# Hashing the first pair of heads with four 32x32 tiles on the array's diagonal

## The chip, the cores and the metric

The kernel runs on one core of one Trainium2 chip. The metric is the device time of one execution in microseconds; several executions of one kernel are summed up by their median.

## What is computed

The reference is hash-masked attention followed by a gated MLP. q, k and v have 4 batches, 8 heads, 768 positions and 64 columns, in fp32. A query and a key may meet only if their hashes agree: each is multiplied by a 64x6 projection, and the six signs are the bucket.

```python
q_bits = (np.einsum('bhsd,dk->bhsk', q, proj) > 0)
k_bits = (np.einsum('bhsd,dk->bhsk', k, proj) > 0)
mask = q_bucket[:, :, :, None] == k_bucket[:, :, None, :]
scores = np.where(mask, scale * np.matmul(q, k.transpose(0, 1, 3, 2)), -1e9)
x = softmax(scores) @ v           # then transposed to 3072 x 512
out = x + sigmoid(x @ w_res) * ((gelu(x @ w_gate) * (x @ w_val)) @ w_out)
```

## The kernel before

**Tiling.** Heads are taken two at a time as a *pair*: 16 pairs, four to a batch. One pair and side (0 for q, 1 for k) is a tile of 128 partitions by 12 chunks of 64 columns (`ld`); chunks 0 to 5 belong to the first head, 6 to 11 to the second. For the scores, each chunk is widened to 71 rows: 64 of data, six of the hash bits as plus or minus one half, and one constant, so that one matmul gives the score with the mask in it. These rows are built in `nat` (bf16, position on the partition) and turned to `aug` (column on the partition).

**Order.** All engines run in the order in which the program issues their instructions; nothing is rearranged by a scheduler. `PLAN` is that order for the first batch, written out by hand, one tuple a step. Its first steps, up to the slots `('S', 0)` and so on, are the start of the kernel. `S` issues one slot of scores: two PSUM banks filled by PE (L500) and one exponential on ACT (L511). There are nine slots a pair. Two PSUM buffers serve all slots in turn, so slot n waits for the exponential of slot n - 2. `V` issues the matmuls with v (L475). After the four pairs of a batch come the gate and value matmuls (L525) and the projections (L557, L571).

**The first pair's path.** Loads come by head on SP's queue (`load_head`, L179): q's first head, k's first, q's second, k's second. The other loads follow on the same queue (L161, L169).

- `cast` writes the 64 data columns of `nat` as bf16: on ACT at L261, on POOL at L263 (q) and L265 (k).
- `tr` (L273, DVE) transposes `ld` in blocks of 32x32 into `t32`: partition 32a + r then holds column r of half a head (32 columns) for the positions of partition group a.
- `hash_one` (L318, PE) multiplies `t32` in fp32 with `projs`. `projs` is block-diagonal, 128x128 for each of the two halves of the head: block a holds 32 rows of the projection in six columns, the rest is zero. Two matmuls, one for each half, sum up in PSUM; the profile shows two matmul instructions for each of them, since fp32 takes two passes.
- `bits_one` (DVE) transposes the sums back in blocks (L323) and writes the six bits into `nat` (L325).
- `turn` (L373, PE) transposes `nat`, chunk by chunk, into a PSUM tile (`pt`), and `copy` moves that to `aug`, on ACT (L379) or DVE (L381).

PLAN takes the first pair in pieces: hash calls for q's chunks 0:4, k's 0:2, k's 2:6, then, after the first `turn` steps, q's 4:6 and 6:12, and k's 6:12 after `('S', 1)`. The `copy` steps for k 0:2, q 0:4 and q 4:6 are on ACT, that for k 2:6 on DVE. The `turn` steps for q 0:4 and q 4:6 write one `pt` tile.

**Where the projection comes from.** It is loaded once, as 32 rows by two halves by six columns (`projn`, L184, on ACT's queue). `spread` (L219, L221) copies it four times into `projs` ('s', two copies on POOL and two on ACT) and four times into `projw` (on POOL). `projw` has the four blocks side by side in 24 of 32 columns. It serves the pairs from 1 on: `hash_mm` (L284) already puts several jobs into column tiles of the array, 128 rows by 32 columns each.

**Before all this** PE runs 52 short matmuls on constants (`fill`, L229), and ACT loads its table of the exponential (L194).

Of the kernel before, what the change touches and what calls it, by code (L numbers as in the profile page):

```python
# [9 lines left out]
FP32 = mybir.dt.float32  # L10
BF16 = mybir.dt.bfloat16
AF = mybir.ActivationFunctionType
# [3 lines left out]

PLAN = [
    ('load', 1, 0), ('load', 1, 1), ('load_v', 0), ('load', 2, 0), ('load_v', 1), ('load', 2, 1),
    ('load', 3, 0), ('proj', 's', 'pssp'), ('proj', 'w', 'pppp'), ('cast', 0, 1, 'p', 0, 6),
# [10 lines left out]
    ('vs', 0), ('load', 4, 0), ('load', 5, 1), ('load', 4, 1), ('load_v', 3),  # L30
    ('S', 0),
    ('S', 1), ('hash1', 0, 1, 6, 12, 'av'), ('bits1', 0, 1, 6, 12), ('turn', 0, 0, 6, 12, 'av'),
# [60 lines left out]
def kernel(  # L93
# [12 lines left out]
    nc = tc.nc  # L106
    B, H, S, D = q.shape
    NBITS = proj.shape[1]
    DMODEL = H * D
    DFF = moe_w_gate.shape[1]  # L110
    P = 128
# [24 lines left out]
    const = ctx.enter_context(tc.tile_pool(name="const", bufs=1))  # L136
# [38 lines left out]
    def load_head(p, side, hi, eng):  # L175
        b, hp = divmod(p, HP)
        if (p, side) not in raw:
            raw[p, side] = ld_pool.tile([P, HT, D], FP32, tag=f"ld{side}", name=f"ld{side}")
        eng.dma_start(raw[p, side][:, hi * T:(hi + 1) * T].rearrange("p t d -> p (t d)"),  # L179
                      (q, k)[side][b, 2 * hp + hi].rearrange("(p t) d -> p (t d)", t=T))  # L180

    load_head(0, 0, 0, nc.sync)
    projn = const.tile([32, 2, NBITS], FP32, name="projn")
    nc.scalar.dma_start(projn, proj.rearrange("(h r) n -> r h n", r=32))  # L184
    load_head(0, 1, 0, nc.sync)
    load_head(0, 0, 1, nc.sync)
    load_head(0, 1, 1, nc.sync)
# [4 lines left out]
    nc.vector.memset(eps_sb, EPS)  # L192
    table = const.tile([P, 1], BF16, name="table")
    nc.scalar.activation(table, warm[:, 0:1], AF.Exp)  # L194
    projs = const.tile([P, 2, P], FP32, name="projs")
    nc.gpsimd.memset(projs, 0.0)
    projr = const.tile([P, NBITS, D], FP32, name="projr")
    projw = const.tile([P, 2, 32], FP32, name="projw")
    nc.gpsimd.memset(projw, 0.0)
# [15 lines left out]

    def spread(dst, engs):
        for a, eng in enumerate(engs):
            if eng is nc.scalar:
                nc.scalar.activation(dst(a), projn, AF.Copy)  # L219
            else:  # L220
                eng.tensor_copy(dst(a), projn)  # L221

    wps, wpt = [sc_ps.tile([P, 1024], FP32, tag="sp", name=name) for name in ("wps", "wpt")]

# [17 lines left out]
    for s in range(3):  # L242
        n = KF // 3
# [11 lines left out]
    def cast(p, side, eng, c0=0, c1=HT):  # L255
        x = (p, side)
        scale = (1.0 / C) if side == 0 else 1.0
        sl = slice(c0, c1)
        dst = nat_of(x)[:, sl, 0:D]
        if eng is nc.scalar:  # L260
            nc.scalar.activation(dst, raw[x][:, sl], AF.Copy, scale=scale)  # L261
        elif side == 0:
            eng.tensor_scalar(dst, raw[x][:, sl], scale, 1.0, op0=ALU.mult, op1=ALU.mult)  # L263
        else:
            eng.tensor_copy(dst, raw[x][:, sl])  # L265

    t32, hsum, htok = {}, {}, {}
# [43 lines left out]
    def hash_one(p, side, c0, c1, tag):  # L311
        n, x = c1 - c0, (p, side, c0)
        if tag in ("w0", "w1"):
            hsum[x] = (wpt, wps)[int(tag[1])][:, 0:2 * n * 32].rearrange("p (i c n) -> p i c n", i=2, c=n)
        else:
            hsum[x] = (av_ps if tag == "av" else mm_ps).tile([P, 2, n, 32], FP32, tag=tag, name="hs1")
        for dh in range(2):
            nc.tensor.matmul(hsum[x][:, 0], projs[:, dh, :], t32[p, side][:, c0:c1, dh, :],  # L318
                             start=(dh == 0), stop=(dh == 1))

    def bits_one(p, side, c0, c1):
        hs = hsum[p, side, c0]
# [52 lines left out]
    def turned(p, side, c0, c1, eng):  # L375
        dst = aug[p, side][0:KA, c0:c1, :]
        pt = pts[p, side, c0 // T][0:KA, c0 % T:c0 % T + c1 - c0]
        if eng is nc.scalar:
            nc.scalar.activation(dst, pt, AF.Copy)  # L379
        else:  # L380
            eng.tensor_copy(dst, pt)  # L381
# [74 lines left out]
    def x_turn(b, hp):  # L456
        pt = mm_ps.tile([P, T, P], BF16, tag="f" if b == 0 else "r", name="pt")
        for t in range(T):
            nc.tensor.transpose(pt[:, t, :], x_tok[b][:, hp, t, :], ident)  # L459
        if hp == HP - 1:  # L460
            nc.scalar.activation(x_sb[b][:, hp, 0:2], pt[:, 0:2], AF.Copy)
            nc.vector.tensor_copy(x_sb[b][:, hp, 2:T], pt[:, 2:T])
        else:
            nc.vector.tensor_copy(x_sb[b][:, hp], pt)
# [124 lines left out]
    ENG = {"v": nc.vector, "s": nc.scalar, "p": nc.gpsimd}  # L589
# [113 lines left out]
    def first_gv(i):  # L703
        begun.append(gv_mm(0, 0, (wg, wv)[i], 0, KM - 1))

    STEP = dict(
        S=score, V=value, fill=fill, tr=tr,
        proj=lambda w, engs: spread(
            (lambda a: projs[32 * a:32 * a + 32, :, 32 * a:32 * a + NBITS]) if w == "s" else
            (lambda a: projw[32 * a:32 * a + 32, :, NBITS * a:NBITS * (a + 1)]),  # L710
            [ENG[e] for e in engs]),
        cast=lambda p, side, e, *c: cast(p, side, ENG[e], *c),
        hash1=hash_one,
        bits1=bits_one,
        turn=lambda p, side, c0, c1, tag: turn_pe(p, side, c0, c1, tag, POOLS[tag]),
        copy=lambda p, side, c0, c1, e: turned(p, side, c0, c1, ENG[e]),
# [4 lines left out]
        w=load_w, load=load, load_v=load_v, xturn=lambda hp: x_turn(0, hp),  # L721
# [10 lines left out]
    for s in range(NSLOT, LAST):  # L732
        p, c = divmod(s, NCH)
# [60 lines left out]
```

## Time and profile before

| | |
|---|---|
| time, median of 3 runs | 339.16 us (339.11 to 339.23) |
| span of the profiled execution | 337.24 us; some 1.9 us of a run lie around it |
| busy: PE, DVE, ACT, POOL | 332.7, 216.4, 213.8, 175.0 us |
| L318, hash of the first pair | 24 matmuls, 3.9 to 10.4 us |
| L284, hash of later pairs | 176 matmuls, from 11.7 us |
| fill, L229 | 52 matmuls, 0.84 to 4.03 us |

The profile is that of one execution; its own run time isn't listed beside the span. Times in it are us from the span's start. In a timeline, a row gives start, length, engine, line, operation, output and input with their shapes and a count; in square brackets stands how long the engine was idle before and what ended that. PE is the matmul, PEld the weight load that belongs to it. Ends of matmuls are modelled, so matmuls that follow one another overlap in the rows; the distance of two starts tells more than the length of one. The columns of the windows view are named where it is shown.

### The profile page before, as it was taken

What the parts mean: (1) busy time and instruction counts of PE and PEld (TensorE: products, weight loads), DVE (VectorE), ACT (ScalarE), POOL (GpSimd) and SP (SyncE); (2) the same over time, 40 slices, a digit from 0 to 9 for tenths busy, and PEclk for the clock granted to TensorE, in tenths of its full rate; (3) what the DMA queues carried; (4) which work ended last, traced back from release to release, by engine and by line L of the source; (5) the groups of instructions that cost most, each with busy time, mean ns of one, the idle gap of its engine ahead of it and who ended that gap; (6) DMA issues with size and microseconds to landing.
All of it is one profiled execution on the core that took longest, in us unless ns stands there. A gap on an engine that the chain in (4) does not pass through costs nothing.

```text
span 337.2 us, 7740 instructions
## 1 busy us (share of the span) xinstructions
PE 332.7 (99%) x3086; PEld 205.2 (61%) x3086; DVE 216.4 (64%) x458; ACT 213.8 (63%) x247; POOL 175.0 (52%) x260
## 2 busy tenths in 40 slices
PE   8999999999999999999999999999999999999996
PEld 8677666565666655665666665666566665666444
DVE  7977675664577958875687896876567444343243
ACT  4889962237999962437999982255999984322220
POOL 4779930234489942575999982567978100000000
PEclk9999999999999999999999999999999999999999
DMA  7998999999966233516149933923140340000012
GB/s 218 372 297 127 207 246 196 188 150 194 319 225 169 61 97 80 106 37 126 63 110 275 268 109 91 137 47 65 32 126 33 80 101 33 31 2 0 31 64 94
DMA packets 74387, 43.88 MB, mean 130 GB/s; under 512 B 52544, under 2 KB 71360, under 8 KB 74352
## 3 DMA queue, kind: packets, MB, share of 16 engines
q1 hardware_dynamic: 67872, 37.95, 45.6%
q0 software_dynamic: 6400, 5.44, 10.4%
q8 instruction: 24, 0.39, 0.5%
q14 instruction: 11, 0.09, 0.1%
q10 hardware_dynamic: 80, 0.00, 0.0%
HBM read 29.56 MB, written 6.29 MB: 106 GB/s over the span
## 4 chain that ended last, share of the span: by engine, by line
PE 93%; ACT 3%; DVE 1%; POOL 1%; issue 1%; DVEq 0%; ACTq 0%
PE sp L525 37%; PE fps L571 18%; PE sp L500 16%; PE av L475 9%; PE rps L557 6%; PE hs L284 3%; ACT ering L511 3%; PE wps L229 1%; PE hs L318 1%; POOL pr L335 1%; PE pt L373 1%; ACT e L511 1%; DVE sums L341 1%; PE pt L459 0%; DVE o L577 0%
## 5 line engine op out<-in xcount | busy, mean ns | idle before, releaser
L511 ACT ACTIVATE e<-sp 128x1024 bf16<-128x1024 f32 x117 | 117.7, 1028 | 8.5 <-PE sp L500 3.4
L335 POOL TENSOR_TENSOR pr<-ld,projr 128x384 f32<-128x384 f32 x96 | 93.9, 998 | 46.3 <-DVE sums L341 27.7
L542 ACT ACTIVATE gt<-sp 128x768 bf16<-128x768 f32 x48 | 38.9, 811 | 83.5 <-PE sp L525 77.9
L500 PE MATMUL sp<-aug,aug 71*128 71x256 bf16 (+1 forms) x384 | 86.0, 325 | 0.3
L571 PE MATMUL fps<-wo,hh 128*128 128x512 bf16 (+2 forms) x312 | 79.6, 362 | 0.0
L545 DVE TENSOR_TENSOR hh<-gt,sp 128x768 bf16<-128x768 bf16 x48 | 45.8, 954 | 44.1 <-PE sp L525 40.8
L525 PE MATMUL sp<-x_sb,wg 128*128 128x512 bf16 (+1 forms) x384 | 70.9, 326 | 0.0
L525 PE MATMUL sp<-x_sb,wv 128*128 128x512 bf16 (+1 forms) x384 | 70.9, 326 | 0.0
L475 PEld LDWEIGHTS <-e 128*128 128x128 bf16 x936 | 43.5, 97 | 25.9
L341 DVE TENSOR_REDUCE sums<-pr 128x6 f32<-128x384 f32 x96 | 50.0, 541 | 11.5 <-POOL pr L335 11.0
L525 PEld LDWEIGHTS <-wg 128*128 128x128 bf16 x384 | 37.1, 98 | 25.6 <-issue 1.2
L525 PEld LDWEIGHTS <-wv 128*128 128x128 bf16 x384 | 37.5, 98 | 24.9 <-issue 0.2
L475 PE MATMUL av<-va,e 128*128 128x65 bf16 x936 | 47.0, 193 | 0.0
L571 PEld LDWEIGHTS <-hh 128*128 128x128 bf16 x312 | 28.1, 97 | 22.0 <-issue 0.2
L500 PEld LDWEIGHTS <-aug 71*128 71x128 bf16 x384 | 29.2, 97 | 11.1 <-issue 2.0
L574 DVE SCALAR_TENSOR_TENSOR fps<-th,fps 128x512 f32<-128x512 f32 (+2 forms) x26 | 17.0, 653 | 26.2 <-PE fps L571 26.0
L557 PE MATMUL rps<-wr,x_sb 128*128 128x512 bf16 x96 | 27.1, 379 | 0.0
L511 ACT ACTIVATE ering<-sp 128x1024 bf16<-128x1024 f32 x27 | 25.8, 1031 | 1.7 <-PE sp L500 1.4
L561 ACT ACTIVATE th<-rps 128x512 f32<-128x512 f32 x24 | 14.2, 594 | 18.5 <-PE rps L557 18.5
L273 DVE STREAM_TRANSPOSE t<-ld 128x768 f32<-128x768 f32 (+3 forms) x28 | 23.1, 844 | 0.7 <-PE hs L284 0.6
L454 DVE COPY av<-av 128x390 f32<-128x390 f32 x24 | 13.5, 563 | 11.9 <-PE av L450 11.7
L263 POOL TENSOR_SCALAR nat<-ld 128x768 bf16<-128x768 f32 (+1 forms) x12 | 9.6, 805 | 20.0 <-DMA aug<-nat 17.4
(76 smaller groups left out, 259.7 us busy)
## 6 DMA issues: line engine op xcount, KB each, us to landing
ldv<-in_v_dram SPq DMA_DIRECT2D x16, 384.0 KB, 5.6
out_dram<-o SPq DMA_DIRECT2D x23, 256.0 KB, 2.4
ld<-in_q_dram SPq DMA_DIRECT2D x15, 384.0 KB, 5.7
ld<-in_k_dram SPq DMA_DIRECT2D x15, 384.0 KB, 6.0
wg<-in_moe_w_gate_dram POOLq DMA_DIRECT2D x4, 384.0 KB, 9.1
wv<-in_moe_w_val_dram POOLq DMA_DIRECT2D x4, 384.0 KB, 10.2
wo<-in_moe_w_out_dram POOLq DMA_DIRECT2D x3, 512.0 KB, 7.5
wr<-in_moe_w_res_dram POOLq DMA_DIRECT2D x1, 512.0 KB, 15.7
```

The source lines that it names most:

```text
L273: nc.vector.transpose(t32[p, side][:, sl].rearrange("p c h n -> p (c h n)"), raw[p, side][:, sl].rearrange("p c d -> p (c d)"))
L335: nc.gpsimd.tensor_mul(pr, raw[x][:, hi * T:(hi + 1) * T], projr[:, bit].unsqueeze(1).to_broadcast([P, T, D]))
L341: nc.vector.reduce_sum(sums[x][:, hi * T:(hi + 1) * T, bit], pr, axis=mybir.AxisListType.X)
L475: nc.tensor.matmul(av[p, hi][:, qt, :], e[:, off:off + P], va[:, hi, jt, 0:D + 1], start=first, stop=(repeats(p, hi) and jt == T - 1), ski ...
L500: nc.tensor.matmul(sp[:, off:off + nq * P], ks[0:KA, hi * T + jt, :], qs[0:KA, hi * T + qt0:hi * T + qt0 + nq, :], start=True, stop=True)
L511: nc.scalar.activation(e, sp, AF.Exp, scale=float(ALPHA))
L525: nc.tensor.matmul(sp[:, c0:c1], w[:, kk, bass.ts(m, P)], xs[:, kk, c0:c1], start=(kk == 0), stop=(kk == KM - 1))
L542: nc.scalar.activation(gt, sp[:, 0:S], AF.Gelu)
L545: nc.vector.tensor_mul(hidden[b][:, m, :], gt, ps[1][:, 0:S])
L557: nc.tensor.matmul(rps, x_sb[b][:, kk, t, :], wr[:, kk, :], start=(kk == 0), stop=(kk == KM - 1))
L571: nc.tensor.matmul(fps[:, cs], hh[:, m, bass.ts(t, P)], wo[:, m, cs], start=(m == 0), stop=(m == KF - 1))
L574: nc.vector.scalar_tensor_tensor(fps[:, cs], th[:, cs], 1.0, fps[:, cs], op0=ALU.add, op1=ALU.mult)
```

## The change

`hash_one` no longer multiplies with a block-diagonal 128x128 matrix. For each half of the head it issues four matmuls of 32x32 weights, tile a at rows 32a and columns 32a of the array, each reading its own 32 partitions of `t32` and writing its own 32 partitions of the sums. The projection is loaded in four copies, one to each group of 32 partitions (`projc`), by two loads on ACT's queue, one for each half; their source repeats the same rows four times. `projs`, its memset and its four spread copies are gone. POOL's copies into `projw` now read `projc`, and come behind the cast of k's chunks 0:6 on POOL. The ACT cast of k's chunks 6:12 moves from its place ahead of the first copies to behind the copy of q's chunks 4:6, just ahead of slot 0.

```diff
-    ('load', 3, 0), ('proj', 's', 'pssp'), ('proj', 'w', 'pppp'), ('cast', 0, 1, 'p', 0, 6),
+    ('load', 3, 0), ('cast', 0, 1, 'p', 0, 6), ('proj', 'pppp'),
     ('cast', 0, 0, 'p', 6, 12), ('tr', 0, 0, 0, 4), ('cast', 0, 0, 's', 0, 6), ('fill', 4, 70),
-    ('cast', 0, 1, 's', 6, 12), ('tr', 0, 1, 0, 2), ('cast', 1, 0, 'p'), ('tr', 0, 0, 4, 6), ('fill', 44, 70),
+    ('tr', 0, 1, 0, 2), ('cast', 1, 0, 'p'), ('tr', 0, 0, 4, 6), ('fill', 44, 70),
...
-    ('bits1', 0, 0, 6, 12), ('tr', 1, 0), ('copy', 0, 0, 4, 6, 's'), ('tr', 1, 1), ('load', 5, 0),
+    ('bits1', 0, 0, 6, 12), ('tr', 1, 0), ('copy', 0, 0, 4, 6, 's'), ('cast', 0, 1, 's', 6, 12), ('tr', 1, 1), ('load', 5, 0),
...
-    projn = const.tile([32, 2, NBITS], FP32, name="projn")
-    nc.scalar.dma_start(projn, proj.rearrange("(h r) n -> r h n", r=32))
+    projc = const.tile([P, 2, 32], FP32, name="projc")
+    for h in range(2):
+        nc.scalar.dma_start(projc[:, h, 0:NBITS], bass.AP(tensor=proj.tensor, offset=proj.offset + 32 * NBITS * h,
+                                                          ap=[[0, 4], [NBITS, 32], [1, NBITS]]))
...
-    projs = const.tile([P, 2, P], FP32, name="projs")
-    nc.gpsimd.memset(projs, 0.0)
+    nc.gpsimd.memset(projc[:, :, NBITS:32], 0.0)
...
-            if eng is nc.scalar:
-                nc.scalar.activation(dst(a), projn, AF.Copy)
-            else:
-                eng.tensor_copy(dst(a), projn)
+            eng.tensor_copy(dst(a), projc[32 * a:32 * a + 32, :, 0:NBITS])
...
         for dh in range(2):
-            nc.tensor.matmul(hsum[x][:, 0], projs[:, dh, :], t32[p, side][:, c0:c1, dh, :],
-                             start=(dh == 0), stop=(dh == 1))
+            for a in range(0, P, 32):
+                nc.tensor.matmul(hsum[x][a:a + 32, 0], projc[a:a + 32, dh, :], t32[p, side][a:a + 32, c0:c1, dh, :],
+                                 start=(dh == 0), stop=(dh == 1), tile_position=(a, a))
```

More of the change, by code (lines that the diff above doesn't have):

```diff
@@ L707 @@
         S=score, V=value, fill=fill, tr=tr,
[L708 to L711, printed above, removed]
+        proj=lambda engs: spread(lambda a: projw[32 * a:32 * a + 32, :, NBITS * a:NBITS * (a + 1)],
+                                 [ENG[e] for e in engs]),
         cast=lambda p, side, e, *c: cast(p, side, ENG[e], *c),
```

## The prediction

> **What bounds the kernel now.** I read the page first, then the busy time by stage.
>
> ```profile
> span 337.2 us, 7740 instructions
> PE 93%; ACT 3%; DVE 1%; POOL 1%; issue 1%; DVEq 0%; ACTq 0%
> ```
> ```profile
> 0.00:8.53 8.53, 7.68 (x85) 7.63 (x85) 6.03 (x23) 3.71 (x8) 3.65 (x18) 1.00 0.76 219
> 8.53:23.70 15.17, 15.13 (x208) 10.54 (x208) 12.68 (x29) 13.10 (x15) 11.44 (x21) 1.00 1.08 348
> 23.70:45.00 21.30, 20.93 (x319) 14.40 (x316) 14.24 (x35) 21.21 (x23) 20.01 (x35) 1.00 0.96 191
> 45.00:337.20 292.20, 288.97 (x2489) 172.64 (x2485) 183.49 (x373) 175.76 (x202) 139.93 (x188) 1.00 0.50 112
> ```
>
> The columns are stretch, length, busy PE, PEld, DVE, ACT, POOL, then clock, DMA share, GB/s. PE looks full everywhere, so the sum says little. The change touches only the first hash, before about 10 us. Behind it ACT is full until 45 us (21.21 of 21.30), and PE after that. Nothing after the start has slack to take up a shift, so the end moves by what the first exponentials move. I therefore look for what sets them, on ACT's timeline:
>
> ```profile
> 7.09 0.52 ACT L261 ACTIVATE nat<-ld 128x384 bf16<-128x384 f32 x1 [2.91 <-DMA ld<-in_k_dram]
> 7.52 0.85 ACT L379 ACTIVATE aug<-pt 71x256 bf16<-71x256 bf16 x2
> L379 ACT ACTIVATE aug<-pt 71x512 bf16<-71x512 bf16 x1 | 0.6, 582 | 0.0
> 8.73 0.38 ACT L379 ACTIVATE aug<-pt 71x256 bf16<-71x256 bf16 x1 [0.36 <-PE pt L373]
> 9.16 3.99 ACT L511 ACTIVATE ering<-sp 128x1024 bf16<-128x1024 f32 x4
> 14.33 1.02 ACT L511 ACTIVATE ering<-sp 128x1024 bf16<-128x1024 f32 x1 [0.91 <-PE sp L500]
> ```
>
> This is the real chain before the first exponential (S0, 9.16). The cast of k's second head waits 2.91 us for a load, two copies (7.52 to 8.37) stand behind it, the transposes of q's chunks 4 and 5 reuse the bank those copies read, and the third copy (8.73) follows them. At the same time PE is nearly as late: I call the six hash calls A (q 0:4), B (k 0:2), C (k 2:6), D (q 4:6), E (q 6:12), F (k 6:12).
>
> ```profile
> L318 PEld LDWEIGHTS wps<-t,projs x4: 333/333/333, 5.5 to 6.2; 128*128 128x128 f32 x4
> L318 PE MATMUL wps<-t,projs x4: 397/421/527, 5.6 to 6.4; 128*128 128x128 f32 x4
> L318 PEld LDWEIGHTS wpt<-t,projs x4: 190/192/192, 6.9 to 7.2; 128*128 128x128 f32 x4
> L318 PE MATMUL hs<-t,projs x16: 314/354/550, 3.9 to 10.1; 128*128 128x192 f32 x8, 128*128 128x128 f32 x4, 128*128 128x64 f32 x4
> ```
> ```profile
> 3.91 1.94 PE L318 MATMUL hs<-t,projs 128*128 128x128 f32 x8
> 5.54 0.97 PEld L318 LDWEIGHTS wps<-t,projs 128*128 128x128 f32 x4
> 6.60 0.52 PE L373 MATMUL pt<-ident,nat 128*71 128x128 bf16 x6
> L373 PE MATMUL pt<-ident,nat 128*71 128x128 bf16 x54 | 4.6, 220 | 0.1
> 6.91 0.53 PEld L318 LDWEIGHTS wpt<-t,projs 128*128 128x128 f32 x4
> 7.41 0.87 PE L318 MATMUL hs<-t,projs 128*128 128x192 f32 x4
> 8.11 0.58 PE L373 MATMUL pt<-ident,nat 128*71 128x128 bf16 x6
> ```
>
> Each call is four passes (two halves of the head by two passes of fp32). C's weight loads (333 ns each, 0.97 for four) are (0.97 - 0.33)/3 = 0.213 us apart; D's (191 ns, 0.53) only (0.53 - 0.19)/3 = 0.113. The same load takes half the time after about 6.6 us, although the granted clock reads 1.00 throughout: PE is slow until then, and A, B and C lie in the slow part. A 64-column pass lasts 314 ns and a 128-column one 421, so 64 columns stream in 0.107 us and 128 columns in 0.213 there. A 128-column pass is thus bound by its data as much as by its weights; only B and D, 64 columns wide, are bound by weights.
>
> **The change part by part.** First, do four diagonal tiles run together? No such matmul is in the trace. The nearest are the column tiles of the later hash:
>
> ```profile
> 21.61 0.37 PE L284 MATMUL hs<-t,projw 128*32 128x192 f32 x4
> 21.61 0.53 PE L284 MATMUL hs<-t,projw 128*32 128x192 f32 x8
> L284 PE MATMUL hs<-t,projw x176: 326/326/350, 11.7 to 207.1; 128*32 128x192 f32 x176
> ```
>
> Four matmuls of 350 ns each fit into 0.37 us, so they run side by side, and the next four end 0.16 us later: a pass of 192 columns costs 0.162 us however many tiles share it. I take the same for diagonal tiles, with a pass bound by its data alone: 0.213 (128 columns, slow), 0.107 (64, slow), about 0.056 (64, fast), 0.162 (192, fast). Bounds: no gain for B and D if 32-column weights come no faster than 128-column ones; four times each pass if the tiles run one after another.
>
> Second, PE changes its tiling. Here the rows show the price:
>
> ```profile
> 21.30 0.38 PE L500 MATMUL sp<-aug,aug 71*128 71x512 bf16 x1
> 13.25 0.49 PE L284 MATMUL hs<-t,projw 128*32 128x192 f32 x4
> 13.68 0.61 PE L500 MATMUL sp<-aug,aug 71*128 71x256 bf16 x3
> ```
>
> Six transposes of 128 bf16 columns, 220 ns each, lie (0.52 - 0.22)/5 = 0.06 apart, the later ones 0.056; 512 columns stream in 0.22. What follows the matmul at 21.30 could start at 21.52; the tiled hash starts at 21.61: 0.09 on the way in. Of the four at 13.25 the last two start at 13.25 + 0.16 and end streaming at about 13.58; S4 starts at 13.68: 0.10 on the way out. The first weights after a switch also lie bare (350 against 326 ns), so I charge 0.12 a switch, up to 0.2 in the slow part. Blocks ABC, DE and F make six switches; four lie ahead of S0, but the first replaces A's own bare weight load (550 against 421 ns, 0.13) and counts nothing.
>
> The sum on PE up to S0: B saves 4 x 0.107 = 0.43. C then ends streaming at 6.17 instead of 6.60. The bits that the first transposes need are no later:
>
> ```profile
> 5.51 0.18 DVE L325 TENSOR_SCALAR nat<-hs 128x24 bf16<-128x24 f32 x1
> 5.89 0.27 DVE L323 STREAM_TRANSPOSE hs<-hs 128x64 f32<-128x64 f32 x1 [0.20 <-PE hs L318]
> 6.19 0.17 DVE L325 TENSOR_SCALAR nat<-hs 128x12 bf16<-128x12 f32 x1
> 6.28 0.57 DVE L273 STREAM_TRANSPOSE t<-ld 128x384 f32<-128x384 f32 x1
> 7.91 0.17 DVE L325 TENSOR_SCALAR nat<-wpt 128x12 bf16<-128x12 f32 x1
> ```
>
> A's bits end at 5.51 + 0.18 = 5.69, and B's transpose waits 0.20 for PE. That wait goes; DVE starts an instruction some 0.08 before the last one's end (its next one after 6.19 + 0.17 begins at 6.28), so B's steps move from 5.89 to 5.61 and its bits are ready at 6.08. Transposes start at 6.17 + 0.15 to 0.2 = 6.36, still slow up to 6.6, and end streaming at 6.81 (before, 6.60 + 6 x 0.056 + 0.02 = 6.96). D starts at 6.93, four passes of 0.056 end at 7.15. E, 192 columns, gains nothing: 4 x 0.162 to 7.80. With the switch the next six transposes run from 7.93 to 8.26, S0 behind them: 8.26 instead of 8.53 (8.11 + 0.58 - 0.22 + 0.06), **0.27 us earlier on PE**. D's bits come at 7.83 (7.91 + 0.17 less 0.25), just in time.
>
> Now ACT. The cast at 7.09 leaves its place, so the first two copies no longer wait for the load (from about 6.7 to 7.6, not 7.52 to 8.37), and the reuse of their bank holds nothing up. The third copy hangs on PE and comes 0.27 earlier, at 8.46. But the cast now stands between that copy and the exponential. One copy of this size holds the next off by 0.27 (the second of the two at 7.52 ends at 8.37 and lasts 0.58, so it starts at 7.79), the cast by 0.43 (7.09 to 7.52). Exponential S0 starts at 8.46 + 0.27 + 0.43 = 9.16; its scores are ready at 8.26 + 0.22 + 0.38 = 8.86. **It starts when it starts now.** The stall on the load is gone, and the work that stood in it is late next. S1 starts 0.27 earlier on PE, F's two switches eat 0.24 of it, S2 is 0.03 earlier. S4 at 14.33 waits for PE's later hash, which follows S3, which waits for exponential S1's buffer: again set by S0. Sum: 0.0, with 0.1 either way for the slow switches.
>
> What costs nothing, and its cover:
>
> ```profile
> 0.80 0.41 ACTq L184 DMA_DIRECT2D projn<-in_proj_dram  x1
> 1.25 1.28 ACT L194 ACT_TABLE_LOAD   x1 [1.25 <-PEq L778]
> 3.65 0.87 POOL L221 COPY projw<-projn 32x12 f32<-32x12 f32 x4
> 5.39 0.51 POOL L263 TENSOR_SCALAR nat<-ld 128x384 bf16<-128x384 f32 x1 [0.30 <-DMA ld<-in_q_dram]
> projn<-in_proj_dram ACTq DMA_DIRECT2D x1, 1.5 KB, 2.3
> ld<-in_k_dram SPq DMA_DIRECT2D x2, 192.0 KB, 3.7
> ```
>
> The second projection load adds 0.41 on ACT's queue, so the table load ends at 2.95, before A at 3.91; the two ACT spread copies that follow go, and the cast of q's first half behind them is wanted only at 6.36. On POOL the cast of k's first half steps ahead of the four projw copies (0.87): even if that half lands as late as the slower row says, at 5.0, its 0.5 is done before 6.36, and projw is first read at 11.7. POOL's two projs copies and the larger memset go. SP's order stays. The projection landed 2.3 us after issue; the second load, issued at 1.21, would land at 3.5 by that, at 4.9 by the slower row. The first load is wanted at 3.9, the second at A's third pass, 4.47. I take the nearest row, 2.3: no wait; by the other end A is 0.4 to 0.6 late. The moved cast's output is read by the transposes of k 6:12, which stand behind the hash at 11.7, 2.5 us after it.
>
> **The rivals.** *Tiles one after another (slower).* The change would then not do what it says. Passes cost four times: A lasts to 7.0 (twelve slow, four fast), B 0.89, C 1.71, D 0.89, E 2.59, with the transposes and switches S0 comes near 14.1 and its exponential at 15.0; F adds 1.9 between S1 and S2. In all 7.8: 347.0 us. Against it speak the column tiles above; for it, that no row has tiles on different rows of the array. The Trainium skill, "TensorEngine Tiling (Array Packing)", Restrictions and Gotchas, says that different row tiles can't use one PSUM bank at the same time, and the diagonal tiles all write one bank; by that rule this is the case, and no row here shows it.
>
> *PE stays slow longer (slower).* PE left the slow rate at 6.6 after running full. With a quarter of the array at work and switches between, it might leave it later. If the slow rate lasted through S0: six transposes 0.64, D 0.43, E 1.28, six more 0.64 and three switches put the last one's end at 9.8 and the exponential at 10.5: +1.4, 340.6 us; a part of it if the delay is shorter. The Trainium skill, "TensorE: Matmul & The Clock Gate", Part 1, ties full clock to a busy window of about 3.4 us that starts anywhere; the trace's 6.6 agrees with such a rule, though the clock row doesn't show it.
>
> *PE turns fast sooner (faster).* Today the load at 7.09 holds the start whatever PE does; afterwards nothing but PE and DVE does. If PE is fast from 4.3, q's second head (landed by 5.39) is transposed by 6.1, the bits of C and D follow by 7.0, the last transposes by 7.6, exponential at 8.3: -0.85, 338.3 us.
>
> *Weights or the load bind.* 32-column weights no faster (B +0.43, D +0.22) or a late projection: +0.6, 339.8 us.
>
> **How the numbers follow.** The span is 337.24 and the median 339.16; the 1.9 us around the span stay. Forecast: 339.1 us, chance 0.57, its own range 338.9 to 339.4. Fast sooner 0.15, weights or load 0.09, slow longer 0.10, one after another 0.09. The range takes in the forecast, fast sooner, the 0.6 and the lesser half of slow longer: 338.2 to 340.3. About 0.2% (0.7 us) is what a measurement of this kernel can tell from no change. Over that on the fast side is half of fast sooner and a little: 0.09; on the slow side one after another, slow longer and a share of the 0.6: 0.22; within: 0.69.
>
> **What would show it.** Right: diagonal matmuls in groups of four that start together; B's passes near 0.11; S0's first matmul near 8.3; the cast between the third copy and the exponential, which starts at 9.1 to 9.2; no ACT wait on a load near 7. Wrong: passes four times as long, an fp32 pass that doesn't halve near 6.6, or an exponential S0 off by more than 0.3. If S0 moves and the end doesn't follow, the chain behind it is misread.

## The result, and the profile after

The changed kernel takes **345.09 us** (median of four runs, 342.42 to 349.10) where the kernel before takes 339.13 on the same chip: ratio 1.0148, 95% interval 1.0112 to 1.0184. One run, 349.10, had PE's clock granted at 0.979 and is left out of the ratio. The forecast was 339.1, the range 338.2 to 340.3: the result lies outside it, on the slow side. The profiled execution took 344.37 us, with a span of 342.3 instead of 337.2.

First the page of the changed kernel: the span, the packets of two queues, and the chain by engine.

```profile
span 342.3 us, 7880 instructions
q8 instruction: 25, 0.41, 0.5%
q10 hardware_dynamic: 264, 0.01, 0.0%
PE 78%; POOL 11%; ACT 3%; DMA 2%; DVE 2%; issue 1%; ACTq 0%; POOLq 0%; DVEq 0%
```

The page of the kernel before has for the same two queues:

```profile
q8 instruction: 24, 0.39, 0.5%
q10 hardware_dynamic: 80, 0.00, 0.0%
```

DMA is now in the chain, q10 (ACT's loads of the projection) carries 264 packets instead of 80, and the engines' own loads of instructions, q8, are one more. All three will matter. Next the chain of waits up to the first exponential (start, length, what):

```profile
0.81 1.18 ACTq L185
1.99 0.03 issue
2.02 5.34 DMA projc<-in_proj_dram
7.36 0.02 issue
```

The projection's second load is issued at 2.0 and lands at 7.36. PE shows what it does meanwhile (start, length, what, and in brackets the idle time before and what ended it):

```profile
3.99 0.65 PE L317 MATMUL hs<-t,projc 32*32 32x128 f32 x8
7.40 0.64 PE L317 MATMUL hs<-t,projc 32*32 32x128 f32 x24 [2.76 <-DMA projc<-in_proj_dram]
8.96 0.83 PE L372 MATMUL pt<-ident,nat 128*71 128x128 bf16 x6 [0.32 <-POOL nat L261]
10.14 1.50 PE L317 MATMUL hs<-t,projc 32*32 32x192 f32 x16
```

A's two passes on the first half run at 3.99, the third waits until 7.40. The second loss stands in the last two rows: six transposes take 0.83 us where they took 0.52, and the sixteen tiles of E 1.50. PE is at half speed again. The windows view (stretch, length, busy PE, PEld, DVE, ACT, POOL, granted clock, DMA share, GB/s) shows it in the clock:

```profile
4.30:7.40 3.10, 0.34 (x9) 0.00 (x1) 0.59 (x3) 0.20 (x1) 0.29 (x1) 1.00 0.95 289
8.10:11.40 3.30, 2.98 (x54) 1.74 (x42) 2.44 (x10) 0.97 (x2) 3.08 (x7) 0.51 1.06 371
```

PE idles for most of 3.1 us, then the granted clock is 0.51 for 3.3. The same view with finer bounds:

```profile
4.78:8.19 3.41, 0.79 (x36) 0.79 (x40) 0.41 (x2) 0.00 (x0) 0.57 (x4) 1.00 0.96 305
8.19:11.60 3.41, 3.09 (x51) 1.68 (x43) 2.35 (x10) 0.97 (x2) 3.23 (x7) 0.50 1.06 366
```

The clock falls at 8.19, not when PE goes idle (2.76 us, up to 7.40) and not when it starts again, and it is back at 11.60. From 7.40 to 8.19 PE ran at the fast spacing, 0.11 us for a pass of 128 columns. On ACT, the rows up to the first exponential:

```profile
12.14 0.38 ACT L378 ACTIVATE aug<-pt 71x256 bf16<-71x256 bf16 x1 [1.73 <-PE pt L372]
12.42 0.51 ACT L259 ACTIVATE nat<-ld 128x384 bf16<-128x384 f32 x1
12.83 1.01 ACT L510 ACTIVATE ering<-sp 128x1024 bf16<-128x1024 f32 x1
```

It starts at 12.83 instead of 9.16: **+3.67**. Of these, 2.93 are A's third pass (7.40 instead of 4.47). The rest of the path, 0.74 longer, has the slow spell in it. Up to the end of the third batch the shift stays at 3.65; between batches three and four 0.25 comes on top (which I didn't follow), and DVE's last result is 3.89 later. But the span is 5.08 longer, so **the tail behind DVE's last result grew by 1.19**, from 2.50 to 3.69 us. The waits of SP's queue in the changed kernel name a part of it:

```profile
SPq L786 <- DMA out_dram<-o: 1.2, 1, 1.2
```

In the kernel before the same row reads 0.3.

### The profile page after: what moved, and what is told of

Read it like the earlier page. It is cut to its first block, busy times and chain, and to the rows that moved or that the text cites. A ratio compares the mean times of both kernels' runs of the same rounds, so it can differ in the third digit from the quotient of the medians.

```text
span 342.3 us, 7880 instructions
## 1 busy us (share of the span) xinstructions
PE 333.4 (97%) x3158; PEld 203.3 (59%) x3158; DVE 216.3 (63%) x458; ACT 213.1 (62%) x245; POOL 174.4 (51%) x258
## 4 chain that ended last, share of the span: by engine, by line
PE 78%; POOL 11%; ACT 3%; DMA 2%; DVE 2%; issue 1%; ACTq 0%; POOLq 0%; DVEq 0%
PE sp L524 36%; PE fps L570 13%; PE sp L499 12%; POOL pr L334 7%; PE av L474 7%; PE rps L556 5%; PE hs L282 3%; ACT ering L510 3%; DMA projc<-in_proj_dram 2%; POOL v L393 1%; PE pt L372 1%; POOL va L385 1%; DMA x_sb<-x_tok 1%; ACT e L510 1%; PE hs L317 1%
## 5 line engine op out<-in xcount | busy, mean ns | idle before, releaser
L541 ACT ACTIVATE gt<-sp 128x768 bf16<-128x768 f32 x48 | 38.9, 810 | 83.8 <-PE sp L524 78.2
L453 DVE COPY av<-av 128x390 f32<-128x390 f32 x24 | 13.5, 564 | 11.9 <-PE av L449 11.7
L419 DVE TENSOR_TENSOR x_tok<-av,rec 128x384 bf16<-128x384 f32 x32 | 17.8, 558 | 1.1
```

The lines of the kernel that those rows point to most:

```text
L419: nc.vector.tensor_mul(x_tok[b][:, hp, :, hi * D:(hi + 1) * D], o[:, 0:T, 0:D], rec.unsqueeze(2).to_broadcast([P, T, D]))
L541: nc.scalar.activation(gt, sp[:, 0:S], AF.Gelu)
```

## The experiments

**Theory:** the four-copy loads land late, since a load whose slowest dimension is 4 goes to four DMA engines. PE then idles and falls to half speed, and the end of the program costs another 1.2 us. **Rivals:** the tiles themselves are slow; many small pieces land late however they are dealt; POOL's new order holds PE.

All versions:

| kernel | first exponential | tail | median | ratio to before, 95% |
|---|---|---|---|---|
| before | 9.16 | 2.50 | 339.13 | |
| the change | 12.83 | 3.69 | 345.09 | 1.0148 (1.0112 to 1.0184) |
| e1 tiles, old load | 8.61 | 3.53 | 340.07 | 1.0029 (1.0019 to 1.0039) |
| e1p the same, cast on POOL | 8.27 | 2.84 | 339.52 | 1.0011 (1.0002 to 1.0020) |
| e2 new load alone | 14.87 | 3.41 | 345.62 | 1.0193 (1.0180 to 1.0207) |
| e3 change, four loads | 11.21 | 3.92 | 343.07 | 1.0098 (1.0063 to 1.0134) |
| e4 change, PE kept busy | 13.07 | 3.30 | 343.94 | 1.0162 (1.0125 to 1.0198) |
| e5 e1p with long fillers | 8.22 | 2.49 | 338.78 | 0.9992 (0.9983 to 1.0001) |
| e6 before, one more load | 9.00 | 3.29 | 339.87 | 1.0030 (1.0017 to 1.0043) |
| e7 before, cast moved | 9.43 | 2.47 | 339.13 | 1.0006 (0.9997 to 1.0014) |
| e9 change, POOL's order | 12.71 | 4.01 | 344.97 | 1.0205 (1.0155 to 1.0254) |
| e11 before, more fillers | 9.49 | 2.47 | 340.36 | 1.0038 (1.0024 to 1.0051) |
| e12 change, other rows | 8.88 | 3.94 | 340.41 | 1.0040 (1.0027 to 1.0053) |

The tail is the time from the end of DVE's last result to the end of the span. First exponential and tail are us of the one profiled execution, the median is that of all runs. The ratio is to the kernel before on the same chip (338.88 to 339.16).

### e2: the new load without the tiles

```diff
-    projn = const.tile([32, 2, NBITS], FP32, name="projn")
-    nc.scalar.dma_start(projn, proj.rearrange("(h r) n -> r h n", r=32))
+    projc = ...          # the change's two loads; projs is filled from it
```

> The kernel before with its 128x128 block-diagonal hash and its cast in place, with one thing of the change: the projection comes in four copies by the two loads, and the block-diagonal weights are copied from those. Theory 'landing': the hash can't start before some 7.4 us, all six calls late, first exponential 12 to 14 us, time 342 to 346, and the executions spread by several us. Theory 'tiles': 339 to 339.5 us.

345.62 us. With the old 128x128 weights the loss is all there, so the tiles don't cause it. Its page has the same packets. In its timeline PE waits for POOL's copy of the projection, which itself waited for the load until 7.32, and its windows show the same clock:

```profile
q10 hardware_dynamic: 264, 0.01, 0.0%
```
```profile
7.82 1.95 PE L320 MATMUL hs<-t,projs 128*128 128x128 f32 x8 [3.79 <-POOL projs L223]
```
```profile
7.40:14.40 7.00, 6.58 (x33) 6.26 (x34) 3.12 (x11) 2.33 (x7) 5.92 (x15) 0.51 1.03 365
```

Here the half clock lasted for 6.8 us, from 7.6 to 14.4.

### e1 and e1p: the tiles on the old load

```diff
-    ('load', 3, 0), ('cast', 0, 1, 'p', 0, 6), ('proj', 'pppp'),
+    ('load', 3, 0), ('proj', 's', 'pssp'), ('cast', 0, 1, 'p', 0, 6), ('proj', 'w', 'pppp'),
...
-    for h in range(2):
-        nc.scalar.dma_start(projc[:, h, 0:NBITS], ...)
+    nc.scalar.dma_start(projn, proj.rearrange("(h r) n -> r h n", r=32))
```

e1p also takes the moved cast off ACT: `('cast', 0, 1, 'p', 6, 12)` behind POOL's cast of the next pair.

> Keeps the 32x32 tiles and the moved cast, but loads the projection once as before (64 pieces of 24 B) and copies it on POOL and ACT into the four groups of partitions. Theory 'landing' (the time is lost because the two four-copy loads land at 7.4 us instead of 3.1): hash starts at 3.9 to 4.0, first exponential at 9.1 to 9.3, time 338.9 to 339.5, and the executions agree to 0.3 us again. Theory 'tiles' (diagonal tiles and switches cost the time themselves): first exponential past 11, time 342 or more.

> As the one before, and the moved cast (k's chunks 6:12) goes to POOL, behind the cast of the second pair's q, so ACT has nothing between the third copy and the first exponential. If the prediction's sum was right (0.27 us gained on PE, eaten by this cast): first exponential near 8.9 instead of 9.16, time 338.7 to 339.0, 0.2 to 0.3 less than the run with the cast on ACT. If the cast is not what holds the exponential: no difference between the two.

The first exponential is 0.55 and 0.89 earlier than before, and yet the times are 340.07 and 339.52. The tails are 1.03 and 0.34 us longer, which gives back all that e1 gained. For e1p it is not the whole account: its profiled run took 338.84, 0.7 less than its median, and what the others spent isn't shown. The difference between the two is 0.55 us, more than expected; of the 1.29 us by which their profiles differ 0.69 lie in the tail. Of the tiles, e1's timeline shows:

```profile
6.60 0.83 PE L319 MATMUL hs<-t,projc 32*32 32x192 f32 x16
```

Sixteen tiles of 192 columns in 0.83 us: (0.83 - 0.32) / 3 = 0.17 us for each group of four, one tile's length 0.32. They run four together: in a group the starts lie 0.007 us apart.

### e12: the same pieces, dealt otherwise

```diff
-        nc.scalar.dma_start(projc[:, h, 0:NBITS], bass.AP(tensor=proj.tensor, offset=proj.offset + 32 * NBITS * h,
-                                                          ap=[[0, 4], [NBITS, 32], [1, NBITS]]))
+        nc.scalar.dma_start(projc[:, h, 0:NBITS], bass.AP(tensor=q.tensor, offset=q.offset + 32 * h,
+                                                          ap=[[D, P], [1, NBITS]]))
```

> The changed kernel with its two loads of 128 pieces of 24 bytes taken from 128 rows of q instead of four copies of the projection, so that the hash is of other numbers (its bits aren't the reference's, and what follows from them); pieces, bytes, queue and place stay. Theory (the copies' outer dimension of 4 deals each load to four engines, and its issue takes 1.18 us): dealt over 16 engines, 8 pieces each, with 256 pieces and 32 writes of semaphores on q10; second load landed at 4.0 to 5.0 instead of 7.36, first exponential 9 to 11, 339.5 to 342 us. Rival (any load of 128 small pieces lands that late, whatever its engines): landed 6.5 to 7.5, first exponential 12 to 13, 344 to 345.5 us.

The view of the DMA issues (packets of the queue; then bytes and time from issue to landing), and ACT's timeline:

```profile
q10 hardware_dynamic: 288, 0.01, 0.0%
projc<-in_q_dram ACTq DMA_DIRECT2D x2, 3.0 KB, 2.3
```
```profile
0.81 0.88 ACTq L185 DMA_DIRECT2D projc<-in_q_dram  x2
8.46 0.51 ACT L259 ACTIVATE nat<-ld 128x384 bf16<-128x384 f32 x1
8.88 1.01 ACT L510 ACTIVATE ering<-sp 128x1024 bf16<-128x1024 f32 x1
```

Landed 2.3 us after issue, 0.88 us for both issues instead of 1.75, first exponential at 8.88, better than expected. The theory stands, against the rival of the small pieces. How the dealing is read: of the 264 packets 256 are pieces of 24 bytes and 8 are semaphore writes of 4 bytes, four for each of the two loads; here there are 32, sixteen for each. In the changed kernel the second load's four writes come at 4.34, 4.78, 4.92 and 7.03 us: three were done before 5, and one was late. In e2, e4 and e9 two of the four come after 5.9. Here all 32 lie between 2.21 and 3.14. The Trainium skill, "DMA: Bandwidth & Descriptors", "Why a DMA increments its semaphore by 16 and not by 1", says that each engine that takes part in such a DMA writes to its semaphore once, and that the DMA goes to the largest number of engines, up to 16, that divides the slowest dimension of both sides; by that, a leading dimension of four copies allows four. The 8 and 32 writes agree.

So the landing, with the shorter issue, is worth some 4 us: 3.7 by the two ratios to the kernel before (1.0148 and 1.0040), 4.2 at DVE's last result in the two profiles (338.63 and 334.42). What is left over the kernel before, 1.25 us by the medians, comes with a first exponential that is 0.28 *earlier*: it is all tail (3.94 against 2.50).

### e3: four loads of 32 partitions

```diff
-    for h in range(2):
-        nc.scalar.dma_start(projc[:, h, 0:NBITS], ...)
+    for a in range(0, P, 32):
+        nc.scalar.dma_start(projc[a:a + 32, :, 0:NBITS], proj.rearrange("(h r) n -> r h n", r=32))
```

> The changed kernel, with the four copies brought by four loads of 32 partitions each (source and destination both 32 rows, 64 pieces of 24 B each, 256 in all as in the change) on ACT's queue. Theory 'four engines' (a load whose source begins with a repeat of four is dealt out to 4 of the 16 DMA engines, 32 pieces in a row on each, between the big loads' pieces): each of the four runs on 16 engines, the last lands near 4.5 us, first exponential 9.2 to 9.8, time 339.2 to 340. Theory 'pieces' (256 small pieces land late whoever carries them): the last lands past 6.5, time 342 or more.

```profile
q10 hardware_dynamic: 320, 0.01, 0.1%
projc<-in_proj_dram ACTq DMA_DIRECT2D x4, 1.5 KB, 3.1
```

256 pieces and 64 writes: sixteen engines a load. The loads landed a median of 3.1 us after issue, but they are issued one after another (0.45 each), so the last tile gets its weights at 5.66. PE runs A in fits and stays slow to 9.3; first exponential 11.21. The landing lies between the two expectations, and the time, 343.07 us, is the rival's: the dealing is right, but the landing is still too late for A. These loads read the same 32 rows four times, as the change does, so reading the same rows again is not what lengthens 3.1 us to the change's 5.3.

### e4: PE kept busy until the load lands

```diff
-    ('tr', 0, 1, 2, 6), ('hash1', 0, 0, 0, 4, 'av'),
+    ('tr', 0, 1, 2, 6), ('fill', 85, 70), ('hash1', 0, 0, 0, 4, 'av'),
```

> The changed kernel with 85 more filler matmuls of 70 columns ahead of hash A, so that PE doesn't idle from 4.3 to 7.4 us while it waits for the projection. Theory (PE falls back to half speed after an idle stretch): PE is fast from about 7 us on and stays so, C's and D's passes and the transposes behind 8.1 us come at the fast spacing (0.056 us for 128 columns of bf16), and the first exponential starts at about 11.7 instead of 12.83. The 170 added instructions also move PE's instruction loads (queue q8, 256 instructions each): the load that fell at 337.5, among the last output transfers, would come some 15 us earlier, and the issue of the second-to-last output DMA take 0.33 us instead of 0.66. Together 1.0 to 1.8 us less: 343.2 to 344.2 us. Rival (the speed goes by something else than PE's own idling): slow spacing from 8.1 to 11.4 as before, first exponential near 12.8, 344.8 to 345.3.

343.94 us, inside what was expected, but not by its sum: the first exponential comes at 13.07, not 11.7. The clock did what the theory says:

```profile
4.30:7.40 3.10, 2.97 (x85) 2.64 (x81) 0.39 (x2) 0.16 (x1) 0.09 (x1) 1.00 0.96 274
8.10:11.40 3.30, 2.31 (x77) 1.53 (x65) 2.66 (x10) 0.86 (x2) 3.08 (x9) 1.00 0.96 327
```

1.00 where it was 0.51, with PE busy in the stretch before. Two things ate it: the projection landed 0.42 later in this execution (7.78), and PE stood for 0.65 us in the middle of E for nothing that the profile shows:

```profile
10.24 0.64 PE hs L317 x15
10.89 0.65 issue
11.54 0.34 PE hs L317
```

What held PE there I didn't settle. Without the two, the first exponential would be at 12.0 (13.07 - 0.42 - 0.65), so the slow spell is worth 0.8 us by this estimate. The median is lower for another reason, the tail (3.30 instead of 3.69).

### e5 and e13: the tail and PE's instruction loads

```diff
-    ('fill', 4, 70), ... ('fill', 44, 70), ('fill', 4, 70),
+    ('fill', 1, 280), ... ('fill', 11, 280), ('fill', 1, 280),
```

> The version of e1p (tiles on one old projection load, the moved cast on POOL) with its 52 fillers of 70 columns made 13 of 280 columns: the same columns, 78 PE instructions fewer. Theory (the end was late because PE's 25th load of instructions fell into the last output transfers, at 332.4 us): that load falls behind the end or is gone, 24 packets on q8, the second-to-last output DMA is issued in 0.33 us instead of 0.50, the tail behind the last DVE result falls from 2.84 to about 2.5 us, and the time by 0.2 to 0.7: 338.8 to 339.3 us. Rival (the tail's length has nothing to do with the instruction loads): 339.4 to 339.7 as e1p, issue still 0.5 or more.

338.78 us, 0.74 below e1p by the medians and 0.6 by the two ratios to the kernel before (the two ran on different chips), with nothing changed but the number and length of the fillers. The theory is right, and the size about right: 0.35 of it is the tail of the two profiles (2.84 and 2.49). What the tail does is read from the traces, record by record:

```
          loads on q8   last of 16 KB at (took)   second-to-last    last output's   tail
                                                  output: issue     semaphore
before        24          322.8  (1.6 us)           0.33 us           110           2.50
e5            24          314.9  (0.9)              0.33              110           2.49
e2            24          329.6  (0.9)              0.33              100           3.41
e6            24          323.5  (1.0)              0.33              100           3.29
e4            25          320.1  (1.0)              0.33              100           3.30
e1            25          333.0  (1.7)              1.07              110           3.53
e1p           25          332.4  (1.4)              0.50              110           2.84
the change    25          337.5  (1.0)              0.66              100           3.69
e9            25          337.7  (1.0)              1.08              100           4.01
e12           25          332.8  (1.6)              0.92              100           3.94
e3            25          335.2  (1.7)              0.97              104           3.92
```

Each load brings 16 KB; the page of the kernel before counts 3086 matmuls and as many weight loads on PE to 24 loads, 257 instructions for each. The tiles add 144 instructions to PE, half a load, and that shifts the loads along the program until one falls into the last output transfers. SP then needs 0.5 to 1.08 us instead of 0.33 to issue the next-to-last of them, and the last one waits. The 78 instructions that the long fillers save take the 25th load away. In e4 the 170 that its fillers add bring it forward to 320.1, and the issue is at 0.33 again: it is the place of the load that counts, not the 25. The Trainium skill, "Runtime: NRT & Kernel Launch", "Instruction fetch mechanics", says that instructions are refilled in blocks of 16 KiB and that crossing one is mostly hidden; the 16 KB agree, and here one was not hidden. The column of the semaphore is explained under e6.

> The version of e5 (tiles, one old load, cast on POOL, long fillers) a second time under the profiler. If the moment at which PE turns fast is the program's own (so far 6.1 to 6.6 in five profiles of kernels with 128x128 weights on one load, 3.8 to 4.4 in three of kernels with tiles on one load and one of the change with more fillers), it comes at 4.0 to 4.4 again and the first exponential at 8.2 to 8.6. If it is chance from execution to execution, it may come anywhere up to 7, and the first exponential then up to 9.3. Tail behind the last DVE result 2.4 to 2.6 us, 24 instruction loads.

The second look shows PE turn fast at 5.2 us where e5 turned at 4.1, first exponential at 8.64, tail 2.49, 338.90 us. So the moment isn't the program's own. The Trainium skill, "TensorE: Matmul & The Clock Gate", Part 1, has a free-running window of about 3.4 us, so that the turn differs from run to run; 4.1 and 5.2 in one kernel and the 3.41 us at 0.50 agree.

### e6: one DMA more

```diff
-    ('S', 24), ('V', 21),
+    ('again',), ('S', 24), ('V', 21),     # loads the projection once more, for nobody
```

> The kernel before with one more 1.5 KB load on SP's queue near 150 us, read by nobody. Theory (each DMA takes the next of eight semaphores, and the end of the program asks for them in a fixed order, so that one more DMA puts the last output on the first of them and the rest of the list is walked after it): the start and the last DVE result as before (9.16 and 334.7), the tail 0.4 to 0.9 longer than 2.50 us, 339.5 to 340.0 us. Rival (the order doesn't matter): 338.9 to 339.3.

339.87 us, +0.95: the start is as before (9.00), the tail 0.79 longer. The records of SP's last waits show why:

```
                       last output DMA        landed   then waits to the drain
before                 334.77, semaphore 110   336.31   none left, drain at 336.39
e6, one load more      334.60, semaphore 100   336.13   103, 105 to 110, drain at 337.04
```

The DMAs take eight semaphores in turn, and the end asks for them in a fixed order, 100 first and 110 last, some 0.06 to 0.4 us for each. In the kernel before the last output happened to have the last one. One more DMA gives it the first, and the whole list is walked after it has landed. The change has one load more. So its tail holds both this and the instruction load. The table under e5 has all four cases: with neither the tail is 2.5, with the semaphore alone (e2, e6, e4) 3.3 to 3.4, with the instruction load alone (e1, e1p) 2.8 to 3.5, with both (the change, e9, e12) 3.7 to 4.0. Side by side they are worth less than the sum.

### e7: the cast alone

```diff
-    ('cast', 0, 1, 's', 6, 12), ('tr', 0, 1, 0, 2), ('cast', 1, 0, 'p'), ('tr', 0, 0, 4, 6), ('fill', 44, 70),
+    ('tr', 0, 1, 0, 2), ('cast', 1, 0, 'p'), ('tr', 0, 0, 4, 6), ('fill', 44, 70),
...
+    ... ('copy', 0, 0, 4, 6, 's'), ('cast', 0, 1, 's', 6, 12), ('tr', 1, 1), ('load', 5, 0),
```

> The kernel before with the moved cast alone. Theory of the prediction (the cast keeps ACT for 0.43 us ahead of the exponentials where PE isn't faster): first exponential 0.2 to 0.5 later than 9.16, 339.3 to 339.7 us. Rival (the cast's old place cost as much, since the first copies stood behind it while it waited for its load until 7.09): 338.6 to 339.1.

```profile
8.73 0.38 ACT L379 ACTIVATE aug<-pt 71x256 bf16<-71x256 bf16 x1 [0.85 <-PE pt L373]
9.02 0.51 ACT L261 ACTIVATE nat<-ld 128x384 bf16<-128x384 f32 x1
9.43 1.01 ACT L511 ACTIVATE ering<-sp 128x1024 bf16<-128x1024 f32 x1
```

The third copy stays at 8.73, the cast keeps ACT for 0.41, the exponential is 0.27 later: the prediction's own term. The time, 339.13 against 338.92, can't be told from no change.

### e9: POOL's order

```diff
-    ('load', 3, 0), ('cast', 0, 1, 'p', 0, 6), ('proj', 'pppp'),
+    ('load', 3, 0), ('cast', 0, 1, 'p', 0, 6),
...
-    ('copy', 0, 0, 0, 4, 's'), ('cast', 1, 1, 'p'), ('hash1', 0, 0, 6, 12, 'av'),
+    ('copy', 0, 0, 0, 4, 's'), ('cast', 1, 1, 'p'), ('proj', 'pppp'), ('hash1', 0, 0, 6, 12, 'av'),
```

> The changed kernel with POOL's four copies of the projection for the later hash put behind its casts instead of ahead of the cast of q's chunks 6 to 11. Theory (POOL's first copy waits for the projection, 7.49, and the cast behind it, 8.45, is late for the transposes at 8.96): the cast runs before 6.5 us, the transposes follow hash C at about 8.65, first exponential 0.2 to 0.4 earlier than 12.83, 344.4 to 345.0 us. Rival (PE would have been no earlier, since DVE's bits or PE's own order hold it): first exponential within 0.1 of 12.83, 345.1 us.

```profile
8.91 0.83 PE L372 MATMUL pt<-ident,nat 128*71 128x128 bf16 x6
```

The transposes now wait for nothing on POOL and still start at 8.91 instead of 8.96. DVE's bits of k 0:2, which they read, set this: they end at 8.76 here and at 8.81 in the change, and the transposes follow 0.15 later in both, as in e5, where they end at 5.65 and PE's row (5.79) names DVE as what ended its wait. DVE's rows in the change and in e9:

```profile
8.64 0.17 DVE L324 TENSOR_SCALAR nat<-hs 128x12 bf16<-128x12 f32 x1
8.59 0.17 DVE L324 TENSOR_SCALAR nat<-hs 128x12 bf16<-128x12 f32 x1
```

First exponential 12.71, of which 0.05 is A's earlier third pass (7.35). My theory falls here: the wait on POOL that the change's row shows ended together with one on DVE.

### e8 and e11: is PE's late turn the 128x128 weights'?

```diff
-    ('fill', 4, 70), ('load_v', 2), ('tr', 0, 1, 2, 6), ('hash1', 0, 0, 0, 4, 'av'),
+    ('fill', 14, 70), ('load_v', 2), ('cast', 0, 1, 'p', 6, 12), ('tr', 0, 1, 2, 6), ('hash1', 0, 0, 0, 4, 'av'),
```

This is e11, with the old place of the cast on ACT empty. e8 is the kernel before, unchanged.

> The kernel before itself, a second execution under the profiler. If PE's late turn to the fast spacing (6.5 us there, 3.8 to 4.4 in the kernels with tiles on one old load) goes with the 128x128 weights, it comes at 6.1 to 6.5 again, and the first exponential at 9.0 to 9.4; if it is chance from execution to execution, it may come near 4, and the first exponential near 8.7. Tail behind the last DVE result 2.4 to 2.6 us in either case, 24 instruction loads on q8.

> The kernel before, 128x128 weights and its one load kept, with ten more fillers ahead of hash A (PE busy to about 4.3 us) and the cast moved to POOL as in e1p. Theory (what the tiles gained at the start came from PE's earlier turn to fast, since at the fast spacing the 128x128 passes cost little more): PE turns fast at 3.8 to 4.4, hash C ends near 5.6, first exponential 8.3 to 8.6, 338.4 to 338.9 us. Rival (with 128x128 weights PE stays slow to 6.1 to 6.5 whatever is ahead): first exponential 9.0 to 9.5, 338.9 to 339.6 us.

Both turn late, at 6.6 and 6.7; even e11's fillers stay at the slow spacing to 4.43, where e4's fillers turned at 3.8. So five profiles of kernels with 128x128 weights on one load turn at 6.2 to 6.7. With tiles on one load or on e12's loads it lies anywhere from 3.6 (e1p) to 5.8 (e12), and e3, where PE stood between the pieces of A, turned at 9.3. Whether the weights have a part in it stays open: e11's PE ran the same fillers as e4's up to 3.8 and didn't turn. The times of these two are not clean: from the 37th to the 73rd exponential e8 took 79.77 us and e11 79.16, all thirteen other profiles 78.2. So the first exponential answers the question here and the time does not. e8's 340.81, a single run, lies 1.93 above the median of the kernel before on its chip (338.88) and carries such a delay of 1.5 us, which I didn't follow.

## Why the prediction was wrong

**The failed step** is the one with which it closed the loads: "the second load, issued at 1.21, would land at 3.5 by that, at 4.9 by the slower row ... I take the nearest row, 2.3: no wait". The load was issued at 2.0 and landed at 7.36, 5.3 us after, far past the slower row. The 2.3 came from a load of 32 rows that goes to sixteen engines, with 16 semaphore writes among q10's 80 packets; the new source's slowest dimension is 4. With the same pieces dealt to sixteen engines (e12), 2.3 us is what one gets. The issue was mis-sized too: the second load "adds 0.41", and both took 1.75 instead of 0.82. The rival "Weights or the load bind" was the right mechanism at a chance of 0.09, and its price, 0.6, should have been some 4.

**What followed from it:** "an fp32 pass that doesn't halve near 6.6" named the slow clock only as a state that PE leaves once. It falls back to it when PE has stood idle, at an estimated cost of 0.8 us here (e4). The Trainium skill, "TensorE: Matmul & The Clock Gate", Part 1, states this too (half rate after one idle window of about 3.4 us), and the prediction used only its other half. The length of the slow spell, 3.41 us, agrees; the idle stretch does not, for it was 2.76 us, and in the 3.41 us before the fall PE was busy for 0.79.

**The end.** "The end moves by what the first exponentials move" held up to DVE's last result: a shift of 2.05 us at the first exponential is 2.03 there in e3, 0.27 is 0.25 in e7, 3.67 is 3.89 in the change. It failed behind that, for a reason that the views of the start can't show. e12 has the landing right and a first exponential 0.28 earlier, and is 1.25 us slower. The change adds a DMA and 144 instructions, and both lengthen the tail. With a landing of 2.3 us the forecast would still have been 1.3 too low.

**What was right:**

- Four diagonal tiles run together: one pass of 192 columns on all four costs 0.17 us, where 0.162 was taken; "one after another" (347.0 us) falls. The Trainium skill, "TensorEngine Tiling (Array Packing)", Restrictions and Gotchas, would not let row tiles share a PSUM bank; the diagonal tiles of e1 all write one bank at that pace.
- ACT's end of the path: third copy, cast, exponential lie 0.28 and 0.41 apart in the changed kernel (0.27 and 0.43 taken).
- "PE turns fast sooner" is what e1, e1p and e5 show at the start, 8.61 to 8.22 against the 8.3 given. So even with the load in time the forecast's own first exponential, 9.16, would not have come (e12: 8.88). It gains 0.8 us up to DVE's last result in e5 (333.93 against 334.74) and 0.4 in its second look, e13, and by the medians less: 338.78 against 338.92.

**The best version**, e5, has the tiles on the one old load, the cast on POOL and long fillers. Its ratio to before is 0.9992 (0.9983 to 1.0001): no difference that these runs can tell.

**Open:** what sets the moment at which PE turns fast; why one or two of the four engines were some 2 us later than the others; what held PE for 0.65 us in e4; the 0.25 us between batches three and four. No run shows a dealing to two engines: e10, meant for it, has no result.

## What to carry to other kernels

Before a load's time is taken from another row, compare the slowest dimension of the two access patterns: one that repeats four copies goes to four engines, and the queue's packet count shows it. A load that PE waits for costs twice, once in the wait and again in the half clock behind it. In a kernel without slack, count the DMAs and the instructions that an edit adds as well, since the program's end can give back what the start gained.

## What the runs showed of the hardware that was not expected

- Issuing a load of 128 pieces with four repeated copies took ACT's queue 1.18 and 0.55 us; with 128 rows instead, 0.39 and 0.45.
- The granted clock shows PE's half speed from 8.19 to 11.60, 3.41 us at 0.50, and in e2 for 6.8 us, twice that. It reads 1.00 in the slow stretch at the very start, which only the spacing of matmuls shows.
- One tiny load with no reader, at mid-kernel, cost 0.95 us (0.79 in the tail of its profile), by the semaphore that it left to the last output.
- A 16 KB load of instructions during the last output transfers made the issue of one of them last 0.50 to 1.08 us instead of 0.33, in six of six kernels.
